# Attention and a feed-forward layer on one core: transposes put with the next scores, and values with scores

## The chip, the cores and the metric

The kernel runs on one core of a Trainium2 chip. The metric is the time of one execution on the device in microseconds (us). Before the change the median of three runs is 831.76 us (831.07 to 832.25).

## The reference

Eight batches, eight heads, 576 positions, head size 64; four heads attend to the last 32 positions ("local"), four to the earlier positions with the same remainder by 32 ("strided"). The result is laid out as 4608 tokens by 512 and goes through two matrices with a gelu (in its sigmoid form) between them.

```
scores = (q @ k.T) / sqrt(64)
scores = where(mask, scores, -1e9)          # heads 0-3: local, 4-7: strided
attn   = exp(scores - max); attn = attn / (sum(attn) + 1e-9)
x      = (attn @ v) as 4608 x 512
h      = x @ w_in                           # 512 x 2048
g      = h * 1 / (1 + exp(-1.702 h))
out    = g @ w_out                          # 2048 x 512
```

## The kernel before

**The products.** Both large matrix products use a scheme of seven products for a 2 by 2 block instead of eight. To keep precision every operand is split into a high and a low part, and a product is three matmuls (high by high, high by low, low by high) for each of two halves of the inner dimension: `product(n, k)` is six matmuls of 128 by 288, into one of six PSUM banks (`m_banks`, mx, my and mz in two sets). `combine(n, k)` takes the product out of its bank on ScalarE or VectorE. Eight blocks of `w_in` by seven products are a pass of 56 slots (`PASS`), two slots apart for one block and interleaved with the next; pass b works on batch b, the first one (batch 0) with plain matmuls (`plain`), which also makes room to prepare the weights.

**The attention.** While pass b multiplies batch b, the attention of batch b + 1 is computed beside it. It comes in pairs: a pair is two pieces of all four heads of one kind, local (96 queries, letter l) or strided (128, letter s), six pairs a batch. The steps of a pair are, with their engines: `scores` (TensorE, into the two banks `s_banks`, s0 and s1), `masked` and `maxima` (VectorE), `below` (GpSimd: minus the maximum), `exps` (ScalarE), `totals` (VectorE: sums and their inverses), `scaled` (GpSimd), `turned` (TensorE: four transposes), `kept` (ScalarE: the copy of the transposed values into the arena), `values` (TensorE) and `moved` (ScalarE: copies into x; four for a strided pair, two for a local one). `turn` is `turned` and `kept` together.

**The order.** Program order is kept strictly on each engine. It is written by hand: `side(s, f, ...)` puts step f behind the product of slot s, and the steps of one slot run in the order in which they were put down. `first(b)` is the slot at which pass b begins. In passes one and two (b = 0 and 1 in the last loop quoted below) the pairs follow each other seven slots apart: pair i has its scores at slot s, its transposes at s + 10, its values at s + 12 (for i = 0, 11 or 10 and 12), and both values and scores use the same banks s0 and s1, from column 0. From batch three on (`groups_of`) two pairs form a group: both scores together, at columns 0 and 256 of the two banks; the first transposes one or three slots ahead of `then`, the second one slot ahead, each into one of the `s_banks`; both values at `then`, into two of the product banks (`v_banks`). The scores of the next group come three slots behind `then`.

**The weights.** In pass one the blocks of `w_in` are made from two words each: `w_scale` and `w_low` (ScalarE), `w_join` (VectorE), `w_high` (ScalarE: the high part, a cast), `w_low_part` (VectorE). In pass two the sums of weight blocks follow, for each block i: `t_load` (DMA), four `t_sum` (GpSimd), `t_high` (ScalarE: a cast) and `t_low` (VectorE), at the slots of the table `sums, high, low`. `half_sums` are four sums on GpSimd for the second matrix, in later passes.

Loads are issued on the SyncE queue by `load_qk` (behind the scores of the pair, or group, before) and `load_v` (behind the values). One helper, line 87, records every operation, so all rows of the profile carry L87, and operations are told apart by their tiles: `arena` holds most data of the attention and the hidden layer, `xa` the split x, `w` a split weight block, `raw` its words, `s` the banks s0 and s1, `ident_sb` marks a transpose, `rinv` the inverse totals.

Of the kernel before, what the change touches and what calls it, by code (L numbers as in the profile page):

```python
# [31 lines left out]
PAIRS = 6  # L32
# [24 lines left out]
def _pairs():  # L57
    out = []
    for b in range(B):
        x = [[(kind, b, U * i) for i in range(PAIRS // 2)] for kind in "ls"]  # L60
        out += x[0] + x[1] if b == 0 else [u for i in range(PAIRS // 2) for u in (x[b < 3][i], x[b > 2][i])]
    return out


def _size(kind):

    return (QL, KL) if kind == "l" else (QS, KS)
# [3 lines left out]
def attn_ffn(ctx, tc, qk, vs, weights, masks, ident, out):  # L71
# [68 lines left out]
    def raw_tile(name):  # L140
# [9 lines left out]
    m_banks = [  # L150
        {x: psum.tile([P, 512], F32, name=f"{x}{i}") for x in ("mx", "my", "mz")} for i in range(2)
    ]
    s_banks = [psum.tile([P, 512], F32, name=f"s{j}") for j in range(2)]

    pairs = _pairs()
# [6 lines left out]
    for j in (1, 2, 3, 0, 4, 5):  # L162
# [3 lines left out]
        t = prs[j].rearrange("p (i m) -> p i m", i=4)  # L166
# [7 lines left out]
    def pr_of(p):  # L174
        return prs[(1, 2, 3, 0, 4, 5)[p] if p < PAIRS else pairs[p][0] == "l"]
# [25 lines left out]
    def windows(kind):  # L201

        if kind == "l":
            return [(BL * w, BL, BL * w, WL) for w in range(3)]
        return [(64 * w, 64, WS * w, WS) for w in range(2)]
# [118 lines left out]
    def turned(p, bank):  # L324
        nq = _size(pairs[p][0])[0]
        for i in range(4):
            transposed(
                bank[:, i * nq : (i + 1) * nq],
                pr_of(p)[:nq, i * 130 + 1 : i * 130 + 129],
                ident_sb[:nq, :nq],  # L330
            )
# [9 lines left out]
    def values(p, banks, at=0):  # L341

        kind, b, c = pairs[p]
        nq = _size(kind)[0]
        v, pt = vts[p], pts[p % 2]
        n0 = QL if kind == "l" else RES[c] * NPOS
        for g in range(2):
            for w, (q0, n, _, nk) in enumerate(windows(kind)):
                if kind == "s":
                    n = min(n0, (w + 1) * WS) - w * WS  # L350
                for u in range(U):
                    i = U * g + u
                    o = g * n0 + (q0 if kind == "l" else w * WS)
                    for j in range(2):
                        slot = j ^ u
                        rows = slice(slot * D, slot * D + nk)
                        matmul(
                            banks[u][j * D : (j + 1) * D, at + o : at + o + n],
                            lhsT=v[rows, i, w, :], rhs=pt[rows, i * nq + q0 : i * nq + q0 + n],
                            start=True, stop=True,  # L360
                        )
        return lambda u, *how: moved(p, u, banks[u][:, at : at + 2 * n0], *how)

    def moves_of(moves):
        for u in range(U):
            for move in moves:
                move(u)

    def moved(p, u, src, copy=scalar.copy, some=(0, 1)):
        kind, _, c = pairs[p]  # L370
        x = {k: xr[k].rearrange("p (g n) -> p g n", g=2) for k in ("11", "12", "21", "22")}
        src = src.rearrange("p (g n) -> p g n", g=2)
        if kind == "l":
            h, o = divmod(c + u, 3)
            copy(out=x[("11", "21")[h]][:, :, o * QL : (o + 1) * QL], in_=src)
            return
        n, r0, half = RES[c], R0[c + u], NPOS // 2
        src = src.rearrange("p g (r t) -> p g t r", r=n)
        for k in some:
            o = x[("12", "22")[k]].rearrange("p g (t r) -> p g t r", r=STRIDE)[:, :, :, r0 : r0 + n]  # L380
            copy(out=o, in_=src[:, :, k * half : (k + 1) * half])
# [235 lines left out]
    def move(i, second, engine):  # L617
        copy = vector.tensor_copy if engine is vector else scalar.copy
        if pairs[i][0] == "l":
            moves[i](second, copy)  # L620
        else:
            for u in range(2):
                moves[i](u, copy, (second,))
# [38 lines left out]
    v, g, c0, c1 = vector, gpsimd, slice(0, 1), slice(1, 2)  # L662
# [21 lines left out]
    def side(s, f, *a):  # L684
        sides.setdefault(s, []).append((f, a))

    def first(b):
        return HEAD + PASS * (b - 1) if b else 0
# [8 lines left out]
    def both_values(p):  # L697
# [4 lines left out]
            load_v(p + i + 2)  # L702
        moves_of(moves)

    def groups_of(b, slots):

        for g in range(3):
            q, s, then = b * PAIRS + 2 * g, slots[g] + 3 * (g > 0), slots[g + 1]
            side(s, both_scores, q)
            for i in range(2):  # L710
                s += 2 * i * (g == 0)
                side(s + i, masked, q + i, s_banks, 256 * i)
                for f, d in (
                    (maxima, 0), (below, 0), (exps, 4), (totals, 5 + (i and g > 0)),
                    (scaled, 5 + (i and g > 0)),
                ):
                    side(s + d + i, f, q + i, s_banks)
                side(then - (3 - (g > 0), 1)[i], turn, q + i, s_banks[i])
            side(then, both_values, q)

    for b in range(B):
        at = first(b)
        if b == 1:
            for t, f, k in ((-11, x_sum, 1), (-10, x_sum, 3), (-9, x_sum, 2), (-6, x_high, 1),
                            (-5, x_low, 1), (-5, x_high, 4), (-4, x_low, 4), (-3, x_high, 0),
                            (-2, x_low, 0), (-1, x_high, 2), (0, x_low, 2), (1, x_sum, 4),
                            (2, x_high, 3), (3, x_low, 3), (4, x_high, 6), (5, x_low, 6),
                            (6, x_high, 5), (7, x_low, 5)):
                side(at + t, f, k, b)
        elif b:  # L730
            c = b == 2
            side(at - 10 - c, x_sum, 1, b)
            side(at - 9 - c, x_sum, 3, b)
            for k in range(7):
                t = at + 2 * k - 6 + (k == 1)
                side(t, x_high, k, b)
                side(t + 1, x_low, k, b)
            side(at - 4, x_sum, 2, b)
            side(at, x_sum, 4, b)
        if 1 < b < B - 1:  # L740
            groups_of(b + 1, [at + t for t in (3, 16, 30, 44)])
        for i in range(PAIRS if b < 2 else 0):
            p = (b + 1) * PAIRS + i
            s = at - 3 * b + 7 * i + 2 * (not b)
            t = ((4, 5, 6, 11, 12) if b else (2, 3, 3, 10, 12)) if not i else (5, 6, 7, 10, 12)
            side(s, scores, p, s_banks)
            side(s, load_qk, p + 2)
            for f, d in ((masked, 0), (maxima, 1), (below, 2), (exps, t[0]), (totals, t[1]), (scaled, t[2])):
                side(s + d, f, p, s_banks)
            side(s + t[3], turn, p, s_banks[0])  # L750
            side(s + t[4], lambda p=p: moves_of([values(p, s_banks)]))
            side(s + t[4], load_v, p + 2)

    def word(f, i):
        f(raws[i])
# [9 lines left out]
            side(at + t, f, i)  # L765
    for i in range(FP):
        load = -15 + i if i < 3 else 7 * i - 20
        sums, high, low = (-12, -4, -1) if not i else (7 * i - 10 + t + (i == 1) for t in (0, 6, 8))
        for m in range(4):
            side(HEAD + sums + (2 if i > 1 and m > 1 else 0), t_sum, i, m)  # L770
        for t, f in ((load, t_load), (high, t_high), (low, t_low)):
            side(HEAD + t, f, i)
# [4 lines left out]
    def stage_views(h):  # L777
        if "stage" not in made:
            made["stage"] = wp.tile([P, WLEN], F32, tag="w", name="stage", bufs=FP + 1)
        t = made["stage"]  # L780
        raw = t[:, :1024].bitcast(U32).rearrange("p (q n w) -> p q n w", q=4, w=2)
        at = 1024 + h % 2 * 896
        return raw, t[:, at : at + 896].rearrange("p (k n) -> p k n", k=7)
# [27 lines left out]
    for h in range(2 * FP):  # L811
        c = first(2 + h // 3) + 8 + 14 * (h % 3) if h < 15 else last - 5
        side(c - 8, half_load, h)
        for t, f in ((0, w_scale), (2, w_low)):
            side(c + t, lambda f=f, h=h: f(stage_views(h)[0]))
        side(c + 4, half_join, h)
        side(c + 5, half_sums, h)
        side(c + 10, half_store, h)

    def landing(h):  # L820
# [193 lines left out]
    for n in range(SETS * NB):  # L1014
        s, q = divmod(n, NB)
# [126 lines left out]
```

## Time and profile before

| | |
|---|---|
| median of three runs | 831.76 us (831.07 to 832.25) |
| the profiled execution, its own time | 831.36 us |
| its span | 829.3 us |
| granted TensorE clock, mean | 1.0 of full speed |
| passes one and two, about | 0 to 130 us |
| stretch with groups, batches three to seven | 150 to 418 us |

How to read it: the span is the part of the execution that the profiler sees, from the first to the last instruction; about 2 us lie around it. Busy shares are of the span. A timeline row merges a run of equal instructions of one engine: its start, the time to the end of the last one, the engine, line, operation, the tile that is written and those that are read, the shape and how many. A matmul's end is modelled, so that rows of TensorE overlap a little; the distance from one start to the next is the safer measure. In brackets stands the idle time of the engine ahead of the row, where there was any, and what ended it.

### The profile page before, as it was taken

The numbers are of one execution on the slowest core, as the hardware profiler recorded it, in microseconds if no ns is written. First come the engines' busy times: TensorE is split into PE (matmuls) and PEld (weight loads), VectorE is DVE, ScalarE is ACT, GpSimd is POOL, SyncE is SP. The second block draws the span as 40 slices with busy tenths as digits, with TensorE's granted clock in tenths as the row PEclk, the third lists the DMA queues.
The fourth block names the chain that finished last, engine by engine and source line by source line (L and its number), as shares of the span: only waits on it lengthen the run. The fifth ranks groups of instructions, "written<-read, shape, count | busy, mean of one in ns | idle before, by whom it ended". The sixth has DMA issues, their size and how long they took to land.

```text
span 829.3 us, 22486 instructions
## 1 busy us (share of the span) xinstructions
PE 818.5 (99%) x9037; PEld 762.1 (92%) x9037; DVE 591.7 (71%) x998; ACT 416.3 (50%) x642; POOL 500.3 (60%) x507
## 2 busy tenths in 40 slices
PE   7999999999999999999999999999999999999998
PEld 5899999999999999999999998889888888898898
DVE  5776877866767658567667876777767776777774
ACT  4666644534444444343446566555555555555550
POOL 4322886433442433233445359999999888888880
DMA  9898775685776775866678954444444444444431
GB/s 340 308 402 314 223 247 182 193 279 191 234 234 198 240 245 173 274 201 225 212 240 245 301 179 127 128 150 131 150 147 134 151 131 132 147 129 127 128 106 48
DMA packets 112504, 164.74 MB, mean 199 GB/s; under 512 B 9744, under 2 KB 88336, under 8 KB 111504
## 3 DMA queue, kind: packets, MB, share of 16 engines
q1 hardware_dynamic: 112400, 163.31, 60.1%
q8 instruction: 71, 1.16, 0.6%
q14 instruction: 33, 0.27, 0.1%
HBM read 104.55 MB, written 58.72 MB: 197 GB/s over the span
## 4 chain that ended last, share of the span: by engine, by line
PE 82%; DVE 2%; POOL 2%; DMA 1%; issue 1%; ACT 1%; SPq 0%; POOLq 0%; DVEq 0%; ACTq 0%
PE my L87 26%; PE mx L87 22%; PE mz L87 20%; PE s L87 14%; POOL arena L87 2%; DMA arena<-stash 1%; DVE arena L87 1%; DVE xa L87 1%; ACT xa L87 0%; DVE ga L87 0%; DVE w L87 0%; SPq L87 0%; ACT arena L87 0%; DVE w_out L87 0%; POOLq L87 0%
## 5 line engine op out<-in xcount | busy, mean ns | idle before, releaser
L87 POOL TENSOR_TENSOR arena<-arena 128x256 f32<-128x256 f32 (+1 forms) x298 | 331.2, 1128 | 119.0 <-ACT arena L87 39.2
L87 DVE TENSOR_TENSOR xa<-arena,xa 128x576 fp32r<-128x576 f32 (+3 forms) x101 | 152.3, 1511 | 42.0 <-ACT xa L87 37.2
L87 PE MATMUL my<-xa,w 128*128 128x288 f32 x1128 | 180.5, 301 | 0.7 <-DVE w L87 0.4
L87 ACT CAST xa<-arena 128x576 fp32r<-128x576 f32 (+3 forms) x103 | 115.3, 1140 | 90.3 <-POOL arena L87 29.4
L87 PEld LDWEIGHTS my<-xa,w 128*128 128x128 f32 x1128 | 156.2, 188 | 3.7 <-DVE w L87 1.0
L87 DVE TENSOR_TENSOR arena<-my,arena 128x288 f32<-128x288 f32 (+1 forms) x224 | 97.6, 443 | 59.1 <-PE my L87 56.3
L87 ACT COPY arena<-mx 128x288 f32<-128x288 f32 (+3 forms) x163 | 55.8, 364 | 158.9 <-PE mx L87 100.4
L87 PE MATMUL mz<-xa,w 128*128 128x288 f32 x804 | 129.9, 298 | 0.0
L87 PE MATMUL mx<-xa,w 128*128 128x288 f32 x804 | 129.6, 298 | 0.0
L87 ACT ACTIVATE arena<-arena 128x1024 f32<-128x1024 f32 (+2 forms) x120 | 105.3, 877 | 41.5 <-POOL arena L87 19.6
L87 POOL TENSOR_TENSOR arena<-arena,nmax 128x432 f32<-128x432 f32 (+1 forms) x42 | 48.2, 1149 | 110.1 <-DVE nmax L87 102.5
L87 PEld LDWEIGHTS mx<-xa,w 128*128 128x128 f32 x804 | 112.9, 188 | 1.0 <-POOL xa L87 0.2
L87 PEld LDWEIGHTS mz<-xa,w 128*128 128x128 f32 x804 | 113.1, 188 | 0.5
L87 DVE TENSOR_TENSOR arena<-mz,arena 128x288 f32<-128x288 f32 (+1 forms) x168 | 73.8, 442 | 37.0 <-PE mz L87 33.0
L87 POOL TENSOR_TENSOR arena<-arena,rinv 96x512 f32<-96x512 f32 (+1 forms) x48 | 51.2, 1067 | 60.9 <-DVE rinv L87 40.8
L87 PE MATMUL mx<-w_out,xa 128*128 128x512 f32 (+1 forms) x378 | 72.2, 317 | 0.0
L87 PE MATMUL mz<-w_out,xa 128*128 128x512 f32 (+1 forms) x366 | 71.4, 321 | 0.0
L87 PE MATMUL my<-w_out,xa 128*128 128x512 f32 (+1 forms) x366 | 71.3, 320 | 0.0
L87 DVE TENSOR_TENSOR ga<-arena,ga 128x1792 fp32r<-128x1792 f32 (+1 forms) x25 | 55.2, 2209 | 20.4 <-ACT ga L87 16.5
L87 PE MATMUL s<-w_out,xa 128*128 128x512 f32 (+1 forms) x378 | 67.7, 321 | 0.0
L87 ACT CAST ga<-arena 128x1792 fp32r<-128x1792 f32 (+1 forms) x25 | 40.8, 1632 | 44.2 <-POOL arena L87 16.0
L87 PEld LDWEIGHTS s<-w_out,xa 128*128 128x128 f32 x378 | 54.9, 188 | 5.8
(81 smaller groups left out, 1092.0 us busy)
## 6 DMA issues: line engine op xcount, KB each, us to landing
hid<-arena SPq DMA_DIRECT2D x256, 144.0 KB, 3.2
arena<-hid SPq DMA_DIRECT2D x144, 256.0 KB, 3.3
arena<-qk SPq DMA_DIRECT2D x23, 448.0 KB, 5.0
arena<-qk SPq DMA_DIRECT2D x21, 472.0 KB, 5.7
arena<-vs SPq DMA_DIRECT2D x23, 384.0 KB, 4.3
out<-arena SPq DMA_DIRECT2D x34, 256.0 KB, 3.6
stage<-w_out SPq DMA_DIRECT2D x16, 512.0 KB, 4.3
raw<-w_in SPq DMA_DIRECT2D x7, 1024.0 KB, 8.9
```

The lines of the kernel that those rows point to most:

```text
L87: ins = call(*args, **kw)
```

## The change

It has three parts.

In `groups_of` the transposes of both pairs of a group stand at slot `then - 3`, into two product banks (`t_banks`), directly followed by the scores of the next group, whose whole chain of steps (`chain`) starts there. Before, the next scores came three slots behind `then`, and so six slots later. The first group of batch three has no group ahead of it and gets its chain at `slots[0]`.

In passes one and two the values of the pairs 0 to 3 come two slots later, where the scores of the pair after next stand, and directly ahead of them; values are written from column 256 on.

Three sets of late steps move: the exponentials, totals, scaling and transposes of some pairs by one or two slots (the tuples `t`), the sums, the high and the low part of weight block 1 (`sums, high, low`: from -2, 4, 6 to -2, 0, 3), and `half_sums` from slot c + 5 to c + 7.

```
+    t_banks = [m_banks[1]["mx"], m_banks[0]["my"]]
+
+    def both_turned(q):
+        for i in range(2):
+            turned(q + i, t_banks[i])
+
+    def chain(s, q):
+
+        side(s, both_scores, q)
+        for i in range(2):
+            side(s + i, masked, q + i, s_banks, 256 * i)
+            for f, d in ((maxima, 0), (below, 0), (exps, 4), (totals, 5 + i), (scaled, 5 + i)):
+                side(s + d + i, f, q + i, s_banks)
+
     def groups_of(b, slots):
 
         for g in range(3):
-            q, s, then = b * PAIRS + 2 * g, slots[g] + 3 * (g > 0), slots[g + 1]
-            side(s, both_scores, q)
+            q, then = b * PAIRS + 2 * g, slots[g + 1]
+            if b == 3 and not g:
+                chain(slots[0], q)
+            side(then - 3, both_turned, q)
             for i in range(2):
-                s += 2 * i * (g == 0)
-                side(s + i, masked, q + i, s_banks, 256 * i)
-                for f, d in (
-                    (maxima, 0), (below, 0), (exps, 4), (totals, 5 + (i and g > 0)),
-                    (scaled, 5 + (i and g > 0)),
-                ):
-                    side(s + d + i, f, q + i, s_banks)
-                side(then - (3 - (g > 0), 1)[i], turn, q + i, s_banks[i])
+                side(then - 3, kept, q + i, t_banks[i])
             side(then, both_values, q)
+            if q + 2 < len(pairs):
+                chain(then - 3, q + 2)
...
-            t = ((4, 5, 6, 11, 12) if b else (2, 3, 3, 10, 12)) if not i else (5, 6, 7, 10, 12)
+            t = ((4, 6, 6, 11, 12) if b else (2, 3, 3, 11, 12)) if not i else (4, 5, 5, 10, 12) if i == PAIRS - 1 and not b else (5, 6, 7, 10, 12)
...
-            side(s + t[4], lambda p=p: moves_of([values(p, s_banks)]))
-            side(s + t[4], load_v, p + 2)
+            then = s + t[4] + 2 * (i < 4)
+            side(then, lambda p=p: moves_of([values(p, s_banks, 256)]))
+            side(then, load_v, p + 2)
...
-        sums, high, low = (-12, -4, -1) if not i else (7 * i - 10 + t + (i == 1) for t in (0, 6, 8))
+        sums, high, low = ((-12, -4, -1), (-2, 0, 3))[i] if i < 2 else (7 * i - 10 + t for t in (0, 6, 8))
...
-        side(c + 5, half_sums, h)
+        side(c + 7, half_sums, h)
```

In the rows of the order below, a tile's number is part of its name (s0_82 is bank s0), the shape is that of the result, and in brackets stand the counts that the instruction waits for, by engine (Activation is ScalarE, Pool is GpSimd) or DMA queue.

TensorE in pass one, before: the last values of pair 1 (128x288 rows are products, 64x32 rows are values, 32x64 rows are scores, here those of pair 3).

```order
L87 MATMUL s0_82<-arena_66 64x32 x2
L87 MATMUL s1_83<-arena_66 64x32 x2
L87 MATMUL my1_80<-xa_67,w_2_706 128x288 x6
L87 MATMUL mz1_81<-xa_67,w_2_706 128x288 x6
L87 MATMUL s0_82<-arena_66 32x64 [waits DMAHW7_49,Activation_49]
L87 MATMUL s1_83<-arena_66 32x64 [waits Activation_49]
L87 MATMUL s0_82<-arena_66 32x64
```

The same place after the change.

```order
L87 MATMUL s0_82<-arena_66 64x32 x2
L87 MATMUL s1_83<-arena_66 64x32 x2
L87 MATMUL s0_82<-arena_66 32x64 [waits DMAHW7_49,Activation_49]
L87 MATMUL s1_83<-arena_66 32x64 [waits Activation_49]
L87 MATMUL s0_82<-arena_66 32x64
```

The two products now stand ahead of the values, and the first scores of each bank, right behind the values, carry a wait for ScalarE.

ScalarE in pass one, before: from the copy of pair 0's transposes (128x512) on; w_2 and raw_3 belong to weight blocks, the four 128x18x6 rows are the copies that empty pair 0's values, the arena row of 96x4x128 is an exponential.

```order
L87 COPY arena_66<-s0_82 128x512 [waits DVE_49,PE_49,Activation_49]
L87 CAST w_2_706<-raw_2_371 128x4x256 [waits DMAHW6_49,DVE_49]
L87 ACTIVATE raw_3_590<-raw_3_590 128x1024 [waits DMAHW3_49]
L87 COPY arena_66<-mx0_76 128x288 [waits DMAHW0_49,PE_49]
L87 COPY arena_66<-s0_82 128x18x6 [waits PE_49,Activation_49]
L87 COPY arena_66<-s0_82 128x18x6 [waits Activation_49]
L87 COPY arena_66<-s1_83 128x18x6 [waits PE_49]
L87 COPY arena_66<-s1_83 128x18x6
L87 ACTIVATE arena_66<-arena_66 96x4x128 [waits Pool_49]
L87 ACTIVATE raw_3_590<-raw_3_590 128x1024
```

The same place after the change.

```order
L87 CAST w_2_701<-raw_2_371 128x4x256 [waits DMAHW6_49,DVE_49]
L87 COPY arena_66<-s0_82 128x512 [waits PE_49]
L87 ACTIVATE raw_3_590<-raw_3_590 128x1024 [waits DMAHW3_49]
L87 COPY arena_66<-mx0_76 128x288 [waits DMAHW0_49,PE_49]
L87 ACTIVATE arena_66<-arena_66 96x4x128 [waits Pool_49]
L87 ACTIVATE raw_3_590<-raw_3_590 128x1024
L87 COPY arena_66<-s0_82 128x18x6 [waits PE_49,Activation_49]
L87 COPY arena_66<-s0_82 128x18x6 [waits Activation_49]
L87 COPY arena_66<-s1_83 128x18x6 [waits PE_49]
L87 COPY arena_66<-s1_83 128x18x6
```

The four copies now stand last of these, behind the exponential and the weight step, and the cast stands first.

TensorE in a group from batch three on, before: the transposes (ident_sb) and the first values (64x32, into mx1).

```order
L87 MATMUL s0_82<-ident_sb_72,arena_66 128x96 [waits Pool_49]
L87 MATMUL s0_82<-ident_sb_72,arena_66 128x96 x3
L87 MATMUL mz1_81<-xa_67,w_3_795 128x288 x6
L87 MATMUL s1_83<-ident_sb_72,arena_66 128x128 [waits Pool_49]
L87 MATMUL s1_83<-ident_sb_72,arena_66 128x128 x3
L87 MATMUL my0_77<-xa_67,w_4_922 128x288 [waits DVE_49]
L87 MATMUL my0_77<-xa_67,w_4_922 128x288 x5
L87 MATMUL mx1_79<-arena_66 64x32 [waits DMAHW7_49,Activation_49]
```

The same group after the change.

```order
L87 MATMUL mx1_79<-ident_sb_72,arena_66 128x96 [waits Activation_49,Pool_49]
L87 MATMUL mx1_79<-ident_sb_72,arena_66 128x96 x3
L87 MATMUL my0_77<-ident_sb_72,arena_66 128x128 [waits DVE_49,Pool_49]
L87 MATMUL my0_77<-ident_sb_72,arena_66 128x128 x3
L87 MATMUL s0_82<-arena_66 32x64 [waits DMAHW5_49]
L87 MATMUL s1_83<-arena_66 32x64
```

Both pairs' transposes now follow each other with no product between them, and the next group's scores follow them, with a wait for their load alone.

## Rows read from the trace of the kernel before

**Rows 1.** The page: busy time, share of the span and instructions by engine

```profile
PE 818.5 (99%) x9037; PEld 762.1 (92%) x9037; DVE 591.7 (71%) x998; ACT 416.3 (50%) x642; POOL 500.3 (60%) x507
```

**Rows 2.** Timeline of TensorE, pass one: start, length, engine, operation, count [idle before]

```profile
47.96 0.90 PE L87 MATMUL s<-arena 64*64 64x32 f32 x48
48.79 1.06 PE L87 MATMUL my<-xa,w 128*128 128x288 f32 x6
49.69 0.95 PE L87 MATMUL mz<-xa,w 128*128 128x288 f32 x6
50.57 0.74 PE L87 MATMUL s<-arena 64*32 64x64 f32 x48
...
52.92 0.95 PE L87 MATMUL mx<-xa,w 128*128 128x288 f32 x6
53.71 0.60 PE L87 MATMUL s<-ident_sb,arena 128*128 128x128 f32 x4
54.06 1.03 PE L87 MATMUL my<-xa,w 128*128 128x288 f32 x6
54.94 0.95 PE L87 MATMUL mz<-xa,w 128*128 128x288 f32 x6
55.82 0.67 PE L87 MATMUL s<-arena 54*64 54x54 f32 x32
...
58.20 0.69 PE L87 MATMUL s<-arena 64*64 64x54 f32 x32
```

**Rows 3.** Timeline of ScalarE, the copies that empty the two values of rows 2

```profile
48.89 0.54 ACT L87 COPY arena<-s 128x192 f32<-128x192 f32 x2
...
56.52 0.65 ACT L87 COPY arena<-s 128x90 f32<-128x90 f32 x4 [0.29 <-PE s L87]
```

**Rows 4.** Timelines of TensorE and VectorE, one group's scores and their first masking

```profile
293.27 1.35 PE L87 MATMUL s<-arena 64*32 64x64 f32 x80
...
294.78 0.75 DVE L87 SCALAR_TENSOR_TENSOR arena<-s,masks_sb 96x256 f32<-96x256 f32 x2 [0.94 <-PE s L87]
```

**Rows 5.** Timelines of VectorE, ScalarE and TensorE: join, first and last ScalarE steps, scores

```profile
37.81 1.41 DVE L87 SCALAR_TENSOR_TENSOR raw<-raw 128x1024 uint32<-128x1024 uint32 x1
...
38.93 0.59 ACT L87 COPY arena<-s 128x512 f32<-128x512 f32 x1 [1.39 <-PE s L87]
...
42.80 1.16 ACT L87 ACTIVATE raw<-raw 128x1024 uint32<-128x1024 uint8 x1
...
42.79 0.69 PE L87 MATMUL s<-arena 64*64 64x54 f32 x32
```

**Rows 6.** Timeline of TensorE, the end of pass one and pass two

```profile
76.53 0.55 PE L87 MATMUL s<-ident_sb,arena 96*128 96x96 f32 x4 [0.47 <-POOL arena L87]
...
94.66 1.34 PE L87 MATMUL my<-xa,w 128*128 128x288 f32 x6
...
97.78 0.51 PE L87 MATMUL my<-xa,w 128*128 128x288 f32 x2
...
99.42 0.69 PE L87 MATMUL s<-arena 54*64 54x54 f32 x32
```

**Rows 7.** Timelines of GpSimd and TensorE: the second pair of a later group

```profile
301.75 1.20 POOL L87 TENSOR_TENSOR arena<-arena,rinv 128x432 f32<-128x432 f32 x1 [0.46 <-DVE rinv L87]
...
302.05 1.04 PE L87 MATMUL mz<-xa,w 128*128 128x288 f32 x6
303.00 0.66 PE L87 MATMUL s<-ident_sb,arena 128*128 128x128 f32 x4
303.41 1.03 PE L87 MATMUL my<-xa,w 128*128 128x288 f32 x6
```

**Rows 8.** Timelines of TensorE and GpSimd: the first group of batch three

```profile
158.29 1.05 PE L87 MATMUL my<-xa,w 128*128 128x288 f32 x6
159.19 0.52 PE L87 MATMUL s<-ident_sb,arena 96*128 96x96 f32 x4
...
159.50 0.92 POOL L87 TENSOR_TENSOR arena<-arena,rinv 128x432 f32<-128x432 f32 x1 [0.40 <-DVE rinv L87]
```

## The prediction

> **What bounds the kernel now.** I read the page first: TensorE is busy for 99% of the span and the next engine, VectorE, for 71% [rows 1]. So I read the rest as one queue, TensorE's, and ask what stands between two products there. The reader is to see in the timeline that a product of six matmuls takes 0.79 us from its start to the next (52.92 to 53.71) and that each piece of attention put between two products costs its own length and a little at the edges: the product behind the values takes 0.90 (48.79 to 49.69) and the one ahead of the scores 0.88 (49.69 to 50.57), so 0.11 and 0.09 us are lost there; ahead of a transpose nothing (52.92 to 53.71), behind one 0.09 (54.06 to 54.94) [rows 2]. The other views, ScalarE's, VectorE's and GpSimd's timelines, I read only where TensorE waits for them, or would.
>
> **Values with scores, passes one and two.** Eight times (pairs 0 to 3 of each pass) the values move two products later and stand directly ahead of the scores of the pair after next. If that were all, the 0.11 and the 0.09 would go: 8 x 0.20 = 1.6 us gained. But the scores go into the same two banks as the values, at other columns, and in the order given above they carry a wait for ScalarE: the count that they wait for is that of the copies which empty these very values. Before, two products (1.58 us) covered those copies; now nothing does. The price from rows: the copies of a strided pair's values start 0.70 us after the values do (55.82, 56.52) and take 0.65, so the scores can start 1.35 behind the values; before it was 58.20 - 55.82 - 1.58 = 0.80. That is +0.55. For a local pair 48.89 - 47.96 + 0.54 = 1.47 against 50.57 - 47.96 - 1.58 = 1.03, +0.44 [rows 2, 3]. Lower bound of each: -0.20, if the wait doesn't hold; upper bound: whatever stands ahead of the copies in ScalarE's queue, below.
>
> On the banks a row and a page speak together. The masking of a group's first pair starts at 294.78, after all 80 score matmuls that began at 293.27, though the first pair's 48 take 0.74 [rows 4]. So an engine here waits for a bank, not for the columns that it needs. The Trainium skill, "PSUM — Partial Sum Buffer", section "PSUM bank collisions raise a hardware error", says the same in general: two engines must be kept apart by bank and quadrant, not by address. The trace agrees; by that rule the eight merges cost 8 x 0.5 = 4 us, and without it they would give 1.6.
>
> The first of the eight is worse. In the first pass the copies now stand behind the exponentials and a whole weight step in ScalarE's queue. Before, seven ScalarE steps ran without a gap from 38.93 to 42.80 + 1.16 = 43.96, 5.03 us; the order now puts the weight cast first, and that one waits for VectorE's join, which ends at 37.81 + 1.41 = 39.22. So the same seven end at about 39.25 + 5.03 = 44.28, and the copies are the last of them: the scores that started at 42.79 start at 44.28, +1.5 [rows 5]. (What the later transpose of this pair saves is in that number already: ScalarE sets it.) Bounds: +0.55 if the cast was ready earlier, +2.5 if the join slips too. For the other three of that pass I take ScalarE as free in time, since TensorE comes 1.5 later by then and the weight steps ahead of the copies do not wait for it; so they cost 0.44, 0.55, 0.44. Sum of pass one: 1.5 + 1.43 = 2.9.
>
> In pass two: 0.55 + 0.44 + 0.55 + 0.44 = 2.0; ahead of its first copies stands a cast that waits for GpSimd's sums; I take 0.5 for it, between 0 and 1.2.
>
> **The moved steps.** The last pair of pass one gets its exponentials, totals and scaling one or two steps earlier; the transposes there stood idle 0.47 us for GpSimd. Gone: -0.5. In pass two a product's six matmuls took 1.34 instead of 0.95 (94.66; it waits for a low part that VectorE now makes ahead of the totals): -0.39. The product at 97.78 takes 1.64 to the values at 99.42, where 0.79 + 0.09 + 0.09 would do: -0.67; the low part of the second weight sum, which it waits for, comes three steps earlier [rows 6]. If these three waits only move, the cost is 1.6 more. Pass two in all: 2.0 + 0.5 - 1.06 = +1.4.
>
> **The groups from batch three on.** Fifteen groups. Here the transposes have banks of their own, the scores banks nobody else uses, so the scores wait for their load alone, and that is issued 14 steps (11 us) ahead. The gain is in waits: in the second and third group of each batch the second transposes start at 303.00, just behind the scaling that ends at 301.75 + 1.20 = 302.95; they take 0.41 where undisturbed ones take 0.35 (53.71 to 54.06), and the product ahead of them 0.95 where 0.79 + 0.09 would do: 0.13 a group, ten groups, -1.3 [rows 2, 7]. The new chain starts six steps earlier and its transposes at most two, so no wait is left. The first group of a batch loses 0.11 ahead of its first transposes (158.29 to 159.19 is 0.90); that goes in four of five, -0.4 [rows 8]. In batch three itself the chain starts where it did and the second transposes come two steps earlier: the scaling that ended at 159.50 + 0.92 = 160.42 comes one step sooner, so ready at about 160.0, while the transposes could go at 159.19 + 0.35 at the latest: +0.5 once [rows 8].
>
> What the merge itself saves is not in the trace: no transposes stand ahead of scores without a wait. Bounds: nothing but what scores cost behind a product, with 0.1 more (+0.1), to all three edges gone (-0.28); fourteen times. I take -0.04: a transpose costs nothing at its front, and only half of the 0.09 behind the first is likely to go; that is -0.6. The rows say why so little: scores pay 0.09 behind a product, transposes nothing. The Trainium skill, "TensorEngine Tiling (Array Packing)", section "Key Properties", says that changing the tiling mode drains the array; transposes use the same 128-row tile as products, scores 64 rows. By that rule the drain ahead of the scores stays whatever stands there, and the trace agrees so far.
>
> Groups: -1.3 - 0.4 - 0.6 + 0.5 = -1.8.
>
> **The sum.** 2.9 - 0.5 + 1.4 - 1.8 = +2.0 us. Against the profiled execution's 831.36 (span 829.3, 2.1 around it) that is 833.4; the median of the three runs, 831.76, lies 0.40 above the profiled one, so 833.8. Behind batch seven TensorE runs on without a wait that this touches, so what is lost stays lost.
>
> **Rivals.** First, faster: the wait for the copies costs nothing, because TensorE reaches the scores after them anyway or the count is met earlier. Then the eight give 1.6 instead of costing 5.4 (1.5 + 1.43 + 2.0 + 0.5), and the sum is -1.6 - 0.5 - 1.06 - 1.8 = -5.0, so 826.8. For it: the columns don't overlap, and that is what the column offset in the code is for. Against: the wait in the order, and rows 4. It decides at the first scores behind values. Chance 0.13.
>
> Second, no change: the stalls are the size I gave, but the two queues ahead of the copies are not there (first pair +0.55, the cast 0). Then 0.55 + 1.43 - 0.5 + 2.0 - 1.06 - 1.8 = +0.6, 832.4. For it: TensorE itself comes later by then, and ScalarE has idle stretches. Against: the seven steps ran without a gap. Chance 0.27.
>
> Third, slower still: the cast that waits for GpSimd's sums holds the copies of all four pairs of pass two, 1.2 us each, 4.8 in place of 0.5: 838.1. Against: behind its first pair the cast starts without a wait. Chance 0.08.
>
> My forecast has 0.52, its own range 832.3 to 835.7 (a half microsecond for each of the two queues, 0.1 for each of eight stalls, 0.7 for the groups). A measurement of this kernel can tell about 0.2%, 1.7 us, from no change: 830.1 to 833.4. The forecast lies just outside; of its chance I put 0.32 above, 0.20 within. With the rivals: slower 0.32 + 0.08 + 0.07 = 0.47, same 0.20 + 0.17 = 0.37, faster 0.13 + 0.03 = 0.16. The range is 829.5 to 836.5: it leaves out the faster rival and the last one.
>
> **What would show it.** In the profile after: eight idle stretches of TensorE ahead of scores in the first 130 us, ended by ScalarE, about 0.7 us each and one of over 2 us; if there are none, the term of 5.4 is wrong. Second transposes of 0.43 or less right behind the first, with no wait for GpSimd from batch four on. No wait ahead of the transposes of the last pair of pass one, and none for the low part of a weight sum. The forecast is wrong if the scores start within 0.2 us of the values' last matmul, or if the span from 150 to 418 us shrinks by other than 1 to 3 us.

## The result and the profile after

The changed kernel takes 840.08 us (median of six, 838.17 to 841.14), the kernel before 831.65 us beside it; the ratio is 1.0092, with a 95% interval of 1.0078 to 1.0107. So it is slower, as forecast, but by 8.4 us instead of 2.0, and outside the range.

The page of the changed kernel, its busy line and the clock by slices; the last line gives the granted TensorE clock in 40 slices, tenths of full speed:

```profile
span 839.2 us, 22487 instructions
PE 819.1 (98%) x9032; PEld 764.9 (91%) x9037; DVE 594.0 (71%) x998; ACT 415.7 (50%) x642; POOL 491.1 (59%) x507
PEclk9999989999999999999999999999999999999999
```

TensorE is busy for about the same time as before (819.1 against 818.5 us [rows 1]) in a span that is 9.9 us longer: most of the loss is waiting, and a part, shown below, is slower work. Matching the start of each product's weight load in the two traces gives where it arises. In the table the difference at product 12 (0.7 us, the start of the execution) is taken off; products 12 to 56 are pass one, 56 to 120 pass two, 120 to 137 the first group of batch three, 137 to 420 the other groups.

| us against the trace before | forecast | measured |
|---|---|---|
| pass one | +2.4 | +2.29 |
| pass two | +1.4 | +7.51 |
| first group of batch three | +0.5 | +1.51 |
| the other fourteen groups | -2.3 | -2.30 |
| sum | +2.0 | +9.0 |

What TensorE waited for between 30 and 130 us, changed kernel (total, times, longest, us):

```profile
PE s L87 <- ACT arena L87: 5.2, 7, 2.4
PE mz L87 <- DVE w L87: 1.2, 1, 1.2
PE my L87 <- DVE arena L87: 0.4, 1, 0.4
PE my L87 <- DVE xa L87: 0.2, 1, 0.2
```

Seven of the eight waits for the copies lie in this stretch, six of about 0.5 and one of 2.4; the eighth comes at 134 us.

The 1.2 us for VectorE belong to the first merge of pass one. A product that used to stand behind the values now stands ahead of them, and reaches the low part of its weight block before VectorE has made it. Behind the values the scores then wait 0.54 us for ScalarE's copies. TensorE, and ScalarE in the last row:

```profile
42.74 0.79 PE L87 MATMUL mz<-xa,w 128*128 128x288 f32 x4 [1.18 <-DVE w L87]
44.69 0.98 PE L87 MATMUL s<-arena 64*64 64x54 f32 x32 [0.54 <-ACT arena L87]
44.24 0.71 ACT L87 COPY arena<-s 128x108 f32<-128x108 f32 x4
```

The long wait stands at the first values of pass two. TensorE's timeline there:

```profile
104.69 0.69 PE L87 MATMUL s<-arena 54*64 54x54 f32 x32
107.80 1.41 PE L87 MATMUL s<-arena 64*64 64x54 f32 x32 [2.42 <-ACT arena L87]
109.14 1.81 PE L87 MATMUL mz<-xa,w 128*128 128x288 f32 x6
110.74 1.64 PE L87 MATMUL my<-xa,w 128*128 128x288 f32 x6
112.18 1.64 PE L87 MATMUL mx<-xa,w 128*128 128x288 f32 x6
113.62 0.67 PE L87 MATMUL s<-ident_sb,arena 96*128 96x96 f32 x4
114.08 1.04 PE L87 MATMUL mz<-xa,w 128*128 128x288 f32 x6
```

ScalarE's queue at the same place:

```profile
106.10 1.04 ACT L87 CAST w<-sums 128x1024 fp32r<-128x1024 f32 x1 [0.86 <-POOL sums L87]
107.05 0.39 ACT L87 COPY arena<-mx 128x288 f32<-128x288 f32 x1
107.34 0.70 ACT L87 COPY arena<-s 128x108 f32<-128x108 f32 x4
```

And the same stretch by windows of 2 us (window, length, busy time and matmuls of TensorE, its granted clock, DMA share, GB/s):

```profile
104.00:106.00 2.00, 1.37 (x38) 1.00 0.89 190
106.00:108.00 2.00, 0.20 (x2) 0.79 0.59 219
108.00:110.00 2.00, 2.00 (x35) 0.50 0.63 180
110.00:112.00 2.00, 2.00 (x10) 0.50 0.78 203
112.00:114.00 2.00, 2.00 (x11) 0.50 0.39 146
114.00:116.00 2.00, 2.00 (x17) 1.00 0.00 0
```

Two things add up. The four copies (107.34) stand behind a weight cast that ScalarE cannot start before 106.10, when GpSimd's sums are ready; TensorE, done with the values at about 105.3, stands idle for 2.42 us. And behind that the granted clock is 0.50, 1.2 in place of 2.4 GHz, for some six us of full work: the products take 1.60, 1.44 and 1.44 us from start to start where 0.89, 0.79 and 0.79 are usual, the scores 1.34 where scores behind such a wait take 0.90 at full clock (105.70 to 106.60 in the kernel with the cast moved, below). Against full speed that is 0.44 for the scores, 0.71, 0.65 and 0.65 for the products and 0.18 for the transposes, 2.6 us.

The groups came out as drawn. One later group of the changed kernel, TensorE, which answers to [rows 7]:

```profile
311.86 0.49 PE L87 MATMUL mx<-ident_sb,arena 96*128 96x96 f32 x4
312.19 0.60 PE L87 MATMUL my<-ident_sb,arena 128*128 128x128 f32 x4
312.72 1.35 PE L87 MATMUL s<-arena 64*32 64x64 f32 x80
```

No wait for GpSimd is left. The scores start 0.53 after transposes that take 0.35 by themselves [rows 2], so standing next to them saves the scores almost nothing; the gain, 0.16 a group, is mostly the wait. In the other kernels below with these groups the same fourteen gain between 2.1 and 2.9 us, so the match with the forecast to the tenth is luck.

### The profile page after: what moved, and what is told of

Read it like the earlier page. It is cut to its first block, busy times and chain, and to the rows that moved or that the text cites. A ratio compares the mean times of both kernels' runs of the same rounds, so it can differ in the third digit from the quotient of the medians.

```text
span 839.2 us, 22487 instructions
## 1 busy us (share of the span) xinstructions
PE 819.1 (98%) x9032; PEld 764.9 (91%) x9037; DVE 594.0 (71%) x998; ACT 415.7 (50%) x642; POOL 491.1 (59%) x507
## 4 chain that ended last, share of the span: by engine, by line
PE 72%; DVE 3%; POOL 2%; DMA 2%; issue 1%; ACT 1%; SPq 0%; POOLq 0%; DVEq 0%; ACTq 0%
PE my L87 22%; PE mx L87 20%; PE mz L87 18%; PE s L87 11%; POOL arena L87 2%; DMA arena<-stash 1%; DVE arena L87 1%; DVE xa L87 1%; DVE w_out L87 1%; DMA arena<-hid 0%; DVE ga L87 0%; ACT xa L87 0%; SPq L87 0%; ACT w_out L87 0%; ACT arena L87 0%
## 5 line engine op out<-in xcount | busy, mean ns | idle before, releaser
L87 DVE TENSOR_TENSOR xa<-arena,xa 128x576 fp32r<-128x576 f32 (+3 forms) x101 | 155.0, 1537 | 41.0 <-ACT xa L87 33.6
L87 PE MATMUL my<-xa,w 128*128 128x288 f32 x1128 | 177.2, 298 | 1.4 <-DVE arena L87 1.0
L87 ACT COPY arena<-mx 128x288 f32<-128x288 f32 (+4 forms) x178 | 63.3, 375 | 200.0 <-PE mx L87 121.0
L87 POOL TENSOR_TENSOR arena<-arena,nmax 128x432 f32<-128x432 f32 (+1 forms) x42 | 44.9, 1069 | 150.9 <-DVE nmax L87 144.4
L87 POOL TENSOR_TENSOR arena<-arena,rinv 96x512 f32<-96x512 f32 (+1 forms) x48 | 49.4, 1030 | 61.9 <-ACT arena L87 30.8
```

The source lines that it names most:

```text
L87: ins = call(*args, **kw)
```

## The experiments

All were timed against the kernel before on the same chip. "By the trace" is the sum of the four stretches of the table above.

**The three parts, each alone.** Groups alone: the other two parts undone.

> The first part alone (transposes with the next scores from batch three on). The trace after the change shows the first group of batch three 1.5 us worse and the other fourteen 2.3 us better. Theory A (the groups did about what was forecast, the excess lies in pass two): 0.8 us under the kernel before, bounds -1.8 to 0. Rival (what the groups show in the changed kernel is a shift that comes from the earlier passes): no difference, or a loss of over 1 us.

830.80 against 832.20 us, ratio 0.9985 (0.9975 to 0.9995); by the trace +0.1, 0, +1.5, -2.7. Theory A holds: the groups gain by themselves, and the first one loses.

Values with scores alone, on the kernel before:

```
-            side(s + t[4], lambda p=p: moves_of([values(p, s_banks)]))
-            side(s + t[4], load_v, p + 2)
+            then = s + t[4] + 2 * (i < 4)
+            side(then, lambda p=p: moves_of([values(p, s_banks, 256)]))
+            side(then, load_v, p + 2)
```

> The second part alone (values of pairs 0 to 3 two slots later, ahead of the next scores). Theory A (the loss is this part's own: copies behind a cast that waits for GpSimd, and the halved clock behind the long wait): +9 us, between 7 and 11, with a wait of 2 us or more at the first scores behind values of pass two and about 6 us at half the clock behind it. Rival B (the moved totals of that pair make GpSimd late, so the long wait needs part three as well): +5, no wait over 1 us, no half clock. Rival C (each of the eight costs more than forecast, evenly): eight waits of about 1.2 us.

840.97 us, ratio 1.0102 (1.0088 to 1.0117): this part is the whole loss, and more. By the trace pass one costs 2.84 (forecast 2.9) and pass two 5.74. Its waits between 90 and 130 us:

```profile
PE s L87 <- ACT arena L87: 3.4, 3, 2.4
PE my L87 <- DVE w L87: 0.4, 1, 0.4
```

And its windows at the long one, with the clock of 0.60 in the second:

```profile
104.00:108.00 4.00, 1.58 (x40) 1.00 0.69 205
108.00:112.00 4.00, 4.00 (x46) 0.60 0.65 211
```

The wait is as long without the moved steps, so rival B falls; one long wait and short ones, so rival C falls. In the changed kernel pass two loses 1.8 more than here: the half clock lasts longer, and 0.35 and 0.20 us of waits for VectorE stand ahead of the values.

Moved steps alone:

> The third part alone (moved steps). The forecast gave it -1.6 us, three waits gone. Theory A, from the changed trace, where the wait ahead of the last transposes of pass one is gone and the two waits for low parts around product 70 are still there: -0.5, between -1 and 0. Rival B (it makes GpSimd late in pass two): a loss of up to 1 us by itself.

831.66 us, ratio 0.9993 (0.9985 to 1.0002): no difference that can be told. By the trace -0.11 in pass one, +0.05 in pass two. The two waits of pass two that the forecast counted as gained (0.39 and 0.67) did not vanish but came up a few products earlier or later; the wait of the last pair of pass one did go, -0.7. In pass one the first pair's later transposes gave most of it back, as TensorE's timeline of this kernel shows:

```profile
38.59 0.60 PE L87 MATMUL s<-ident_sb,arena 128*128 128x128 f32 x4
38.94 1.04 PE L87 MATMUL mx<-xa,w 128*128 128x288 f32 x6
41.00 0.69 PE L87 MATMUL s<-arena 54*64 54x54 f32 x32 [1.01 <-ACT arena L87]
```

To test that, the same with one number put back (the part of its line that differs):

```
-((4, 6, 6, 11, 12) if b else (2, 3, 3, 11, 12))
+((4, 6, 6, 11, 12) if b else (2, 3, 3, 10, 12))
```

> The moved steps alone, but with the transposes of the first pair of pass one at their old slot. In the trace of the moved steps alone, moving them lost 1.46 us and gained 0.6 (the copy of these transposes stands behind the weight cast, and the values wait 1.0 us for it). Theory A: 0.9 us less than the moved steps alone in the trace between products 12 and 20, the wait of 1.0 us gone, time 1.0 to 1.5 under the kernel before. Rival (the cast is late anyway): no difference from the moved steps alone.

831.85 us, ratio 0.9993 (0.9983 to 1.0002). By the trace pass one gains 0.71 instead of 0.11 and the wait of 1.01 is gone, but the transposes wait 0.40 for GpSimd instead, as in the kernel before. Between products 12 and 20 it is 0.4 less than with the moved steps alone, where 0.9 was expected: the theory is right in kind, but its size was too large, and the effect is too little to show in the time.

**The long wait.** First, only the first pair of pass two as before:

```
-            then = s + t[4] + 2 * (i < 4)
+            then = s + t[4] + 2 * (i < 4 and (not b or i > 0))
```

> The changed kernel with only the first pair of pass two as before (its values at their old slot), seven merges left. Theory A: the 5.4 us that open there go, wait and half clock: about +3.0 over the kernel before, between 2 and 4. Rival C (the loss is spread over the eight): +7.3.

837.64 us (835.11 to 840.22), ratio 1.0060 (1.0040 to 1.0079), +5.4 by the medians, outside the 2 to 4 that was expected. By the trace pass two costs 2.75 instead of 7.51, and the sum is +4.0. The missing part is in the next pair, whose scores now wait 1.34 us in place of 0.41, for copies behind the next cast of the same kind. TensorE, and below it ScalarE:

```profile
111.40 0.90 PE L87 MATMUL s<-arena 64*64 64x32 f32 x48
113.64 0.93 PE L87 MATMUL s<-arena 64*32 64x64 f32 x48 [1.34 <-ACT arena L87]
114.50 1.05 PE L87 MATMUL mz<-xa,w 128*128 128x288 f32 x6
115.39 0.95 PE L87 MATMUL my<-xa,w 128*128 128x288 f32 x6
```

```profile
112.02 1.04 ACT L87 CAST w<-sums 128x1024 fp32r<-128x1024 f32 x1 [0.92 <-POOL sums L87]
```

Behind 1.34 us of waiting the clock stayed full here (114.50 to 115.39 is 0.89).

Then only the cast moved, by one slot, so that it stands behind the copies:

```
+        high += i == 2
```

> The changed kernel with one ScalarE step moved by a slot: the cast of weight sum 2, which waits for GpSimd's sums, now stands behind the copies that empty the first values of pass two. Theory A (that cast holds the copies): the wait shrinks from 2.4 us to the 0.6 of the other merges, the clock stays at full speed, the time falls by about 4.9 us, to +3.5 over the kernel before. Rival D (the copies are late for another reason, TensorE or VectorE): the wait stays over 1.5 us and the time within 1 us of the changed kernel.

836.16 us (835.74 to 836.25), ratio 1.0046 (1.0033 to 1.0058), +4.05 by the medians, where 3.5 was expected. By the trace pass two costs 3.02. TensorE in this kernel:

```profile
104.51 0.69 PE L87 MATMUL s<-arena 54*64 54x54 f32 x32
105.70 0.97 PE L87 MATMUL s<-arena 64*64 64x54 f32 x32 [0.50 <-ACT arena L87]
106.60 1.06 PE L87 MATMUL mz<-xa,w 128*128 128x288 f32 x6
107.49 0.95 PE L87 MATMUL my<-xa,w 128*128 128x288 f32 x6
```

One ScalarE step moved by a slot takes 4.5 of the 7.5 us away: the wait falls from 2.42 to 0.50 and no product is slow. The cast is the cause, and rival D falls.

**The clock by itself.** Matmuls that nobody reads, behind the values and ahead of the copies, so that TensorE works through the wait (`busy` is true for the first pair of pass two alone):

```
...
+                for _ in range(14 if busy else 0):
+                    matmul(
+                        s_banks[0][:, :256], lhsT=wv[2][:, 0, 0, :128], rhs=xv[0][:, 0, 0, :256],
+                        start=True, stop=True, skip_group_check=True,
+                    )
...
```

> The changed kernel with 14 matmuls of 128x256, whose result nobody reads, behind the first values of pass two, so that TensorE works through most of the long wait, which stays as long. Theory A (the idle stretch makes the clock fall to half, and that costs 3.0 us beside the wait itself): the clock stays at full speed and the time falls by 3 us, to +5.4 over the kernel before. Rival E (the slow products behind the wait have another cause, such as their weights or the DMA traffic of that stretch): the time stays, or rises by up to 0.5 us.

The clock stayed at full speed there and TensorE was 2.4 us ahead by product 76 (2.7 with the difference at product 12 left in), but the time was 839.46 us, ratio 1.0084 (1.0069 to 1.0098), only 0.6 us less than first measured for the changed kernel, or 1.1 with each against its own runs of the kernel before; 1.1 us were given back in waits near 477 us. So both were run together, the filled wait with 18 such matmuls:

> The changed kernel once more, so that it stands beside the filled wait below under the same conditions. +8.4 us over the kernel before, as first timed; bounds +7 to +10.

> The changed kernel with 18 matmuls of 128x256, whose result nobody reads, behind the first values of pass two (the first such kernel had 14, and 0.58 us of idle time were left; its clock stayed full, TensorE was 2.7 us ahead by product 76, but 1.1 us of that were given back near 477 us, in waits for late weights, and the timed gain was 0.6). Theory A (the halved clock costs 2.7 us, and what is missing in the time is lost to later waits that differ from run to run): TensorE ahead by 2.5 to 3 us at product 76 and again at product 390, time 1 to 2.7 us under the changed kernel of these runs. Rival (the half clock is worth nothing in the time, since something else sets the end): the time within 0.5 us of the changed kernel.

The changed kernel: 841.98 us, ratio 1.0110 (1.0091 to 1.0129). The filled wait: 838.99 us, ratio 1.0084 (1.0064 to 1.0105). TensorE with the filled wait:

```profile
105.19 0.69 PE L87 MATMUL s<-arena 54*64 54x54 f32 x32
105.80 2.42 PE L87 MATMUL s<-xa,w 128*128 128x256 f32 x18
108.72 0.99 PE L87 MATMUL s<-arena 64*64 64x54 f32 x32 [0.49 <-ACT arena L87]
109.63 1.05 PE L87 MATMUL mz<-xa,w 128*128 128x288 f32 x6
...
112.38 1.04 PE L87 MATMUL mz<-xa,w 128*128 128x288 f32 x6
```

From the scores to the product behind the transposes (108.72 to 112.38) it is 3.66 us; in the changed kernel above (107.80 to 114.08) it is 6.28, and 6.25 in its second trace: the half clock costs 2.6 us, and it comes from the idle time, since the weights and the loads are the same. By the trace TensorE is 1.9 ahead at product 120 (the added matmuls hold the copies up by 0.4) and 2.0 at product 420, less than the 2.5 to 3 that was expected. Of the eleven executions of the changed kernel in these two series one shows a mean granted clock of 1.000 (838.17 us, the fastest of them), of the eleven with a filled wait six: the clock seems to fall in most executions of the changed kernel, but not in each. The medians differ by 3.0 us, but the two intervals overlap, so for the time itself the size is not settled better than "some 1 to 3 us". The Trainium skill, "TensorE: Matmul & The Clock Gate", section "Part 1: The HAM clock gate", says that the slow clock is the resting state and that activity releases it; the two traces agree, with 0.50 behind 2.42 us of idle time and 1.00 where matmuls filled it.

**Without the second part, and with it in other banks.** The changed kernel with values at their old slots (`2 * (i < 4)` to `0 * (i < 4)`):

> The changed kernel without its second part: values at their old slots in passes one and two, the groups and the moved steps kept. Theory A: groups -0.8 and moved steps -0.5 add up to 1.3 us under the kernel before, between -2.5 and 0. Rival B (the moved steps carry part of the loss): above the kernel before.

830.93 against 832.11 us, ratio 0.9983 (0.9974 to 0.9992). By the trace -0.9. Theory A holds.

Then with pass two's values merged again, but into two product banks that are idle there:

```
+            then = s + t[4] + 2 * (b == 1 and i < 4)
+            side(then, lambda p=p, o=b == 1 and i < 4, j=i % 2: moves_of([
+                values(p, (m_banks[j]["mx"], m_banks[1 - j]["mz"]) if o else s_banks)
+            ]))
```

> The kernel without the second part, but with the values of pairs 0 to 3 of pass two merged with scores as in the change, written into two product banks that are idle there instead of the banks of the scores. Theory A (the merge costs because the scores wait for the bank to be emptied, not because values and scores stand together): no wait ahead of those scores, four edges of 0.2 us less than without the merge, 2 us under the kernel before. Rival F (the copies stay late, and now the next product in that bank waits for them): the first merge of pass two still shows a wait of over 1 us, ahead of a product, and the time is 1 us or more above that without the merge.

830.88 us, ratio 0.9986 (0.9977 to 0.9995), the same as without the merge. The third merge, its last values and its scores:

```profile
118.48 0.23 PE L87 MATMUL mz<-arena 54*64 54x36 f32 x2
118.52 0.67 PE L87 MATMUL s<-arena 64*64 64x54 f32 x32
119.12 1.06 PE L87 MATMUL mz<-xa,w 128*128 128x288 f32 x6
```

The scores follow the values with no wait, and the second to fourth merge gain 0.20, 0.33 and 0.24 us each by the trace, against losses of 0.46, 0.68 and 0.44 in the changed kernel. The first loses about 0.5, in products that wait or run long (from product 70 to 77 it is +0.12 here and -0.43 without the merge), so a part of rival F is true too, and the 2 us under the kernel before that were expected did not come. In the second to fourth merge, then, what costs is the shared bank: the forecast's bounds of a merge, -0.20 and about +0.5, are both measured now. The Trainium skill, "PSUM — Partial Sum Buffer", section "PSUM bank collisions raise a hardware error", says to guard accesses by bank and quadrant, not by address. The order of this program does so, and the runs agree: other columns of the same bank leave the wait, another bank takes it away. What the chip would do without that wait no run here shows.

**The first group.** A first attempt gave no usable time (the expectation below says why). The second (`late` is true for the first group of batch three alone):

```
...
+                side(then - 3, turn, q, t_banks[0])
+                side(then - 1, turn, q + 1, m_banks[0]["mz"])
...
+                chain(then - 3 + 2 * late, q + 2)
...
```

> The groups as in the change, but in the first group of batch three the second transposes stand two slots later, and the next chain of scores behind them (in the kernel before this one the next chain's masking came ahead of these transposes and wrote over the probabilities that they read, so that its result and its time say nothing); of the moved steps only those of the last pair of pass one; values and scores as before. Theory A (the first group's 1.5 us are the wait of its second transposes for GpSimd's scaling): -2.3 for fourteen groups, about 0 for the first, -0.7 for the last pair, 3.0 us under the kernel before, between 2 and 3.5, and the trace shows no loss between products 103 and 137. Rival (the first group loses because the next chain, now later, holds its own transposes): the loss comes up at the second group instead, 1.5 us under.

830.91 against 832.23 us, ratio 0.9984 (0.9970 to 0.9999); the first group costs 0.78 instead of 1.51. So the theory is half right, and the time, 1.3 us under the kernel before, misses the 2 to 3.5 that was expected. By the trace pass one gains only 0.21, and pass two loses 0.88, much of it in two waits of 0.19 and 0.57 us for the split x near 90 us, which stand in other traces too (other banks, filled wait). The rest of the first group's loss stands earlier, in this kernel's timeline too:

```profile
157.82 1.03 PE L87 MATMUL my<-xa,w 128*128 128x288 f32 x6 [0.69 <-DVE arena L87]
```

A product waits 0.69 us because VectorE empties its bank late. In the changed kernel VectorE's row shows why: the masking and the maxima of the second pair now stand directly behind those of the first, ahead of that copy:

```profile
162.24 0.93 DVE L87 SCALAR_TENSOR_TENSOR arena<-s,masks_sb 96x256 f32<-96x256 f32 x2
...
163.81 0.66 DVE L87 SCALAR_TENSOR_TENSOR arena<-s,masks_sb 128x216 f32<-128x216 f32 x2
164.50 0.60 DVE L87 TENSOR_REDUCE nmax<-arena 128x8 f32<-128x432 f32 x1
...
166.64 0.44 DVE L87 TENSOR_TENSOR arena<-my,arena 128x288 f32<-128x288 f32 x1
```

The pair's steps come two slots earlier than before, 1.3 us of VectorE's work ahead of the emptying at 166.64; the product follows at 167.23. That was read, not tried. Four kernels (groups alone, without the merge, other banks, first group apart) beat both; they lie within 0.2 us of each other, at about 1.2 to 1.4 us under the kernel before.

## Why the prediction was right or wrong

**The step that failed** is the term of pass two: "ahead of its first copies stands a cast that waits for GpSimd's sums; I take 0.5 for it, between 0 and 1.2". Measured by moving that cast it is 4.5 us: some 1.9 of waiting, above its own bound, and 2.6 of half clock, which no term had. The rows for the first half were there. In the trace before the cast starts at

```profile
102.43 1.05 ACT L87 CAST w<-sums 128x1024 fp32r<-128x1024 f32 x1 [0.87 <-POOL sums L87]
```

and the values start at 99.42 [rows 6]; two products later they end at 99.42 + 1.58 + 0.62 = 101.62, so the cast would hold the copies from there to 103.4, 1.8 us. I had reckoned the cast's own length and not the moment at which its input is ready. The delay from pass one gave no slack either: GpSimd's sums came later with it, and the cast started at 106.10. The third rival had the right engine and the right queue, but four waits of 1.2, where one of 2.4 and three short ones came. Without the first merge the second pair's cast did hold its copies, for 1.34 us.

**The moved steps** were the second miss: -1.56 forecast, -0.1 measured over the two passes. The price for "these three waits only move" stood beside it and was the truth for two of the three. That is why pass two still costs 3.02 us with the cast moved: the forecast's 2.0 for the four merges, 0.4 lost in products 60 to 70 (0.35 with the moved steps alone), and the two waits of 0.35 and 0.20 us for VectorE ahead of the values, with no gain against them.

**Right** were the wait itself, which the order showed, and its price: pass one +2.29 against +2.4, alone +2.84 against 2.9; the first merge there 1.53 against 1.5 (ScalarE's copies end at 44.24 + 0.71 = 44.95, which is the 44.28 of the forecast with the later start of 0.67), the other three 0.44, 0.60 and 0.42 against 0.44, 0.55 and 0.44. Right too were the fourteen groups, -2.30 against -2.3, with the gain mostly in the waits and next to none in the merge; that the tenth agrees is luck. The first group's +0.5 was one wait (0.55 seen); the other, VectorE's 0.7, was missed.

**Of the signs that were named**, eight waits of about 0.7 and one over 2 us came as seven of about 0.5 and the one of 2.4; the latter stood in pass two, not in pass one, where 1.18 us were spent ahead of the values already, in the wait for VectorE. The stretch with groups shrank by 0.8 us (2.30 less 1.51), outside the 1 to 3 that was named. The wait of the last pair of pass one is gone, the second transposes follow at 0.33 without a wait. The first rival (no wait at all) is excluded by the 5.2 us.

## What to carry to other kernels

When a step moves ahead, ask of every instruction that is queued in front of its helper not how long it takes but when its input is ready, and follow that input back to the engine that makes it. A wait of TensorE can cost more than its length: here 2.42 us of it brought 2.6 us of half clock behind it. And where the order keeps waits by bank, as in this program, two uses of one accumulation bank that follow each other directly wait for the engine that empties it, whatever columns they use.

## What was not expected of the hardware

Behind 2.42 us of idle time TensorE ran some 6 us at a granted clock of 0.50, in both traces of the changed kernel, and some 3 us with values and scores alone; behind 1.34 us of idle time, without the first merge, it did not fall. These two lengths are no threshold: in seven traces of the experiments the granted clock also fell to 0.50 once in the first 24 us, where TensorE waits for loads again and again. With the cast moved it was 0.50 from 15.5 to 18.8 us, with no single wait over 0.92 us in the 10 us ahead of it, but TensorE busy for only 2.7 of the 4.4 us from 11.0 to 15.4. That stretch lies ahead of product 12 and is in no sum above.

Scores behind a transpose started 0.18 us later than a product would have (0.53 at 312.19, against 0.35 [rows 2]), more than the 0.09 they pay behind a product.
